# Attention, pooled, then a SiLU block: a new prologue by 256 positions, two seven-product units in the first tile, and loads in another order

## The chip, the core and the metric

One core of a Trainium2 chip runs the whole kernel. The metric is the device time of one execution in microseconds; three runs of the kernel before gave 278.92, 278.94 and 279.31 (median 278.94). A core has five engines that run side by side and meet at semaphores: TensorE (PE: matmuls, with PEld for its weight loads), VectorE (DVE), ScalarE (ACT), GpSimd (POOL) and SyncE (SP). Matmuls write to PSUM, which has eight banks of 512 float32 columns. Transfers between HBM and SBUF are started by SP, ACT and POOL.

## What is computed

```
q, k, v: (8, 8, 576, 64) float32            # batch, head, position, dim
k_p, v_p = mean of k, v over groups of 8 positions     # 72 pooled positions
scores = q @ k_p^T / 8
attn   = softmax(scores)                                # over the 72
x = (attn @ v_p), heads side by side: (4608, 512)
h = x @ w_in                                            # w_in: (512, 2048)
g = h * sigmoid(h)
out = g @ w_out                                         # w_out: (2048, 512), out (4608, 512) float32
```

## The kernel before

The 4608 rows of x are worked in nine tiles of 512. A tile has a first product (x with `w_in`, then SiLU into `h_T`) and a second product (`h_T` with `w_out`, then the store). The attention of batch t+1 is worked inside tile t, so only batch 0 has to be worked ahead of everything; this is the prologue. All is in bfloat16 but for PSUM, the raw k and v and a few sums.

*Order.* The order on each engine is written out by hand: instructions stand on an engine in the order in which the program issues them. Inside a tile a generator `spread` counts steps of PE work, and fillers (attention work, sums, loads) have a step behind which they are issued. An instruction that waits holds all that stands behind it on its engine.

*Banks.* PSUM has the pools "mm" (three banks) and "at" (five).

*Attention of a batch.* k and v come in as rows in five slots of up to 128 rows by 512 float32 (`load_slots`); `slot_sums` adds the eight positions of a group (three adds on DVE for slots 0 to 2, three for 3 and 4); `select_k` and `select_v` bring the sums into place with small matmuls, `copy_k` and `copy_v` take them out of PSUM. `q_transpose` turns q on DVE. `scores` multiplies four heads at a time in four groups of rows of the array, and ACT takes the exponentials (L338) into `es`. `denominators` sums them with a matmul; ACT takes the logarithm (L357) and the exponential of its negative (L358), or DVE the reciprocal (L354). `numerators` multiplies with v (L374), and DVE multiplies with the reciprocal into `xT` (L383). In the prologue this is done in four parts: two groups of four heads (g) by two halves of 288 positions (f). Matmuls on zeros (`warm_up`, L708) stand between the steps.

*First product of tile 0* (`up`). Groups 0 to 10 of 128 columns of `w_in` are worked on the first 288 positions, then on the other 224, then groups 11 to 15 on all 512 (`plain`, L474). The denominators and numerators of the second half stand among the first groups.

*Second product of tile 0* (`down`, L509). Row blocks m = 0, 1, 2 of 128 rows are worked side by side over the 16 groups, then m = 3. The attention of batch 1 stands among them, by thirds of 192 positions.

*Units.* From tile 1 on most of both products is done by seven products of half-blocks instead of eight. They need sums of blocks of x (`unit_x_sum`), of `w_in` (`unit_weight_sum`, one set for each of four units a, b, c, d) and of `w_out` (`weight_sum`); products 1 to 7 go to three banks A, B and E, and DVE and ACT add between them (`behind`). A unit covers four groups. In tile 0 no unit is used; the sums are made in its second product.

*Loads.* k of batch 0 is started by SP and ACT, all else by POOL in this order: q first half, v slots 0 to 2, q second half, v slots 3 and 4, `w_in` columns 0 to 1535 (six transfers), k of batch 1, the last 512 columns of `w_in` (two), q of batch 1, three quarters of `w_out`, v of batch 1, the last quarter of `w_out`.

```python
    act_copy = nc.scalar.copy
    warm_up(9)
...
    q_transpose(0, 0, 0)
    scores(0, part(0, 0))
...
            items = [(g, 0, HS) for g in range(GA)]
            items += [(g, HS, NTT - HS) for g in range(GA)]
            items += [(g, 0, NTT) for g in range(GA, KG)]
            f_up += [(1, lambda: denominators(0, part(0, 1), on_dve=True))]
```

Of the kernel before, what the change touches and what calls it, by code (L numbers as in the profile page):

```python
# [32 lines left out]
ALU = mybir.AluOpType  # L33
# [3 lines left out]
def kernel(  # L37
# [47 lines left out]
    psum = ctx.enter_context(  # L85
        tc.tile_pool(name="psum", bufs=1, space=bass.MemoryType.PSUM)
    )
    ctx.enter_context(tc.manual_schedule())
    banks = dict(mm=3, at=5)

    def ps_tile(shape, dtype, tag, name):
        return psum.tile(shape, dtype, tag=tag, bufs=banks[tag], name=name)
# [18 lines left out]
    w_sum1 = [  # L111
        singles.tile([128, 4, 2, 256], BF16, name=f"w_sum1{n}") for n in range(len(UNITS))
    ]
# [9 lines left out]
    def load_q_half(b, f):  # L123
        for a in range(2):
            es = slice(f * QF * D, (f + 1) * QF * D)
            nc.gpsimd.dma_start(out=batches[b]["q_bf"][:, a, es], in_=q_r[b][:, a, es])
# [22 lines left out]
    def q_transpose(b, a, f):  # L149
        st = batches[b]  # L150
        n = QF * D
        nc.vector.transpose(
            out=st["qT"][:, a, f * QF : (f + 1) * QF]
            .rearrange("r i p c -> r (i p c)").bitcast(FP32),
            in_=st["q_bf"][:, a, f * n : (f + 1) * n].bitcast(FP32),
        )
# [91 lines left out]
    def slot_sums(name, j, halves=False):  # L248
        raw = row_tiles[name][j]
        dst = rows5[name][:, SA:] if j else rows5[name][:, :SA]  # L250
        w = RE // 4 if halves else RE // 2
        while w > D:
            nc.vector.tensor_add(  # L253
                out=raw[..., :w], in0=raw[..., :w], in1=raw[..., w : 2 * w]
            )
            w //= 2
        nc.vector.tensor_add(out=dst, in0=raw[..., :D], in1=raw[..., D : 2 * D])
# [10 lines left out]
    def select_k(b, a):  # L268
        st = batches[b]
        if a == 0:  # L270
            st["kz_ps"] = ps_tile([128, 2, 2, SP], FP32, "at", "kz_ps")
# [26 lines left out]
    def copy_v(b, a, copy=nc.vector.tensor_copy):  # L298
        hs = slice(4 * a, 4 * (a + 1))
# [4 lines left out]
    def part(g, f):  # L304
        return ((g, f * QF, (f + 1) * QF),)
# [16 lines left out]
    def scores(b, segs):  # L322
        st = batches[b]
        w = width(segs)
        sc = [ps_tile([128, 512], FP32, "at", "sc_ps")[:SP, :w] for s in range(4)]
        for g, i0, i1, cs in seg_cols(segs):
            for c in range(2):
                for s in range(4):
# [3 lines left out]
                        lhsT=kz[b % 2][rows, g, c, :],  # L332
                        rhs=st["qT"][rows, g, i0:i1, :, c],
                        start=(c == 0), stop=(c == 1),
                    )
        es = mid.tile([SP, 4, VW], BF16, tag="es", bufs=4, name="es")[:, :, :w]
# [5 lines left out]
    def denominators(b, segs, on_dve=False):  # L342
        st = batches[b]
        w = width(segs)
        es = st["es", segs]
        den_ps = ps_tile([128, 512], FP32, "at", "den_ps")
# [5 lines left out]
        rec = mid.tile([128, VW], FP32, tag="rec", bufs=4, name="rec")[:, :w]  # L352
        if on_dve:
            nc.vector.reciprocal(rec, den_ps[:, :w])  # L354
        else:
            lnd = mid.tile([128, VW], FP32, tag="lnd", name="lnd")[:, :w]
            nc.scalar.activation(lnd, den_ps[:, :w], func=AF.Ln)  # L357
            nc.scalar.activation(rec, lnd, func=AF.Exp, scale=-1.0)  # L358
        st["rec", segs] = rec

    def numerators(b, segs, tags=("at", "at")):
# [6 lines left out]
        rec = st.pop(("rec", segs))  # L368
        nu = []
        for c in range(2):  # L370
            nu_ps = ps_tile([128, 512], FP32, tags[c], "nu_ps")
            for g, _, _, cs in seg_cols(segs):
                for s in range(4):
                    nc.tensor.matmul(  # L374
                        nu_ps[32 * s : 32 * (s + 1), cs],
                        lhsT=st["vp"][:, 4 * g + s, c::2],
# [5 lines left out]
        for c in range(2):  # L382
            nc.vector.tensor_mul(  # L383
                out=xT[:, 2 * g0 + c : 2 * (g0 + ng - 1) + c + 1 : 2, cols],
                in0=nu[c][:, :w].rearrange("r (g n) -> r g n", g=ng),
                in1=rec.rearrange("r (g n) -> r g n", g=ng),
# [41 lines left out]

# [531 lines left out]
```

## Time and profile before

| what | value |
|---|---|
| median of three runs | 278.94 us |
| the profiled execution's own time | 278.04 us |
| its span, from first to last instruction | 276.3 us |
| k of batch 0, slots 0 to 2, summed on DVE | 5.22 to 7.16 us |
| first matmul of the first product | 16.36 us |
| first matmul of the second product of tile 0 | 32.76 us |
| first matmul of tile 1 | 51.03 us |
| bytes moved by DMA, 0 to 60 us | 14.23 MB, 237 GB/s |

A row of the timeline has the start, the duration, the engine, the line, the operation, what it writes and reads, the shape and the count, and in brackets the engine's idle time ahead of it with what ended it; like instructions in a row are merged. A row of the groups has the count, the busy time, the mean ns of one and the idle time ahead. Matmul durations overlap: the pace is read from the distance of their starts. A row of the table of stretches has its bounds, its length, each engine's busy time and count in the order PE, PEld, DVE, ACT, POOL, and then the granted clock of PE, the busy share of the DMA engines and what they moved.

### The profile page before, as it was taken

How to read it: one execution, taken by the hardware profiler on the slowest of the kernel's cores; microseconds unless marked ns; L12 is line 12 of the kernel's file. 1: busy time of each engine (PE TensorE's matmuls, PEld its weight loads, DVE VectorE, ACT ScalarE, POOL GpSimd, SP SyncE). 2: the span in 40 equal slices, each digit the busy share in tenths (PEclk: the TensorE clock that was granted, in tenths of full speed). 3: DMA queues.
4: the chain of work that ended last, by engine and by line, in shares of the span. 5: the costliest groups of instructions: out<-in, count | busy, mean ns of one | idle time of the engine just before them, and what ended most of it. 6: DMA issues, size and time to landing. Idle time of an engine off the chain costs nothing.

```text
span 276.3 us, 7291 instructions
## 1 busy us (share of the span) xinstructions
PE 270.6 (98%) x2959; PEld 211.3 (77%) x2959; DVE 209.7 (76%) x388; ACT 190.7 (69%) x376; POOL 97.3 (35%) x102
## 2 busy tenths in 40 slices
PE   8999999999999999999999999999999999999994
PEld 4348544488788878887888778877887788888883
DVE  4887886887997877877787787768787786766872
ACT  1678766568669785979497958895798578409710
POOL 8756216252138620962087229851900000000000
PEclk9999999999999999999999999999999999999999
DMA  7999999896757896569556966999410032004104
GB/s 211 285 253 246 207 321 180 245 184 117 152 62 147 220 167 116 137 168 169 103 111 170 171 109 159 186 107 132 124 31 0 4 87 67 4 19 110 26 2 152
DMA packets 31473, 37.72 MB, mean 137 GB/s; under 512 B 10352, under 2 KB 22384, under 8 KB 31440
## 3 DMA queue, kind: packets, MB, share of 16 engines
q0 software_dynamic: 23792, 26.64, 52.5%
q1 hardware_dynamic: 7216, 9.97, 13.1%
q10 hardware_dynamic: 432, 0.66, 0.7%
q8 instruction: 23, 0.38, 0.6%
q14 instruction: 10, 0.08, 0.1%
HBM read 36.70 MB, written 9.44 MB: 167 GB/s over the span
## 4 chain that ended last, share of the span: by engine, by line
PE 93%; DVE 4%; DMA 2%; issue 0%; DVEq 0%
PE o_psB L608 16%; PE u_psB L589 15%; PE o_psA L608 10%; PE o_psE L608 10%; PE u_psA L589 10%; PE u_psE L589 10%; PE hp_ps L474 7%; PE sc_ps L330 4%; PE o_ps L509 4%; PE nu_ps L374 3%; PE den_ps L348 2%; DMA raw<-in_k_dram 2%; PE warm_ps L708 1%; DVE xT L383 1%; DVE w_sum L548 1%; DVE raw L253 1%
## 5 line engine op out<-in xcount | busy, mean ns | idle before, releaser
L608 PEld LDWEIGHTS <-h_sum 128*128 128x128 bf16 x512 | 48.4, 98 | 8.8 <-issue 1.2
L589 PEld LDWEIGHTS <-w_sum 128*128 128x128 bf16 x496 | 48.2, 98 | 5.7
L338 ACT ACTIVATE es<-sc_ps 72x384 bf16<-72x384 f32 (+1 forms) x100 | 39.0, 469 | 12.2 <-PE sc_ps L330 12.1
L608 PEld LDWEIGHTS <-h_T 128*128 128x128 bf16 x384 | 36.6, 98 | 6.1 <-issue 1.1
L589 PEld LDWEIGHTS <-w_in_sb 128*128 128x128 bf16 x372 | 36.3, 98 | 4.4
L589 PE MATMUL u_psA<-xT,w_in_sb 128*128 128x256 bf16 x248 | 37.4, 273 | 0.0
L589 PE MATMUL u_psB<-x_sum,w_sum 128*128 128x256 bf16 x248 | 36.7, 273 | 0.0
L608 PE MATMUL o_psB<-w_sum,h_sum 128*128 128x256 bf16 x256 | 32.7, 273 | 0.3 <-DVE o_psE L623 0.3
L608 PE MATMUL o_psA<-w_out_sb,h_T 128*128 128x256 bf16 x256 | 31.9, 272 | 0.0
L618 DVE COPY u_psB<-u_psA 128x512 f32<-128x512 f32 x31 | 21.4, 698 | 10.5 <-PE u_psA L589 10.3
L623 DVE TENSOR_TENSOR u_psE<-u_psB,p 128x512 f32<-128x512 f32 x31 | 20.9, 693 | 9.7 <-ACT p L621 8.6
L627 ACT ACTIVATE h_T<-u_psE 128x512 bf16<-128x512 f32 x31 | 18.5, 598 | 11.2 <-PE u_psE L589 10.9
L383 DVE TENSOR_TENSOR xT<-nu_ps,rec 128x384 bf16<-128x384 f32 (+1 forms) x50 | 23.8, 530 | 0.2
L183 POOL TENSOR_TENSOR raw<-raw 72x1024 f32<-72x1024 f32 x10 | 23.6, 2361 | 0.0
L640 DVE TENSOR_TENSOR c<-u_psB,p 128x512 f32<-128x512 f32 x31 | 21.0, 681 | 3.1 <-PE u_psB L589 2.3
L537 DVE TENSOR_TENSOR h_sum<-h_T 128x1024 bf16<-128x1024 bf16 (+1 forms) x31 | 21.3, 698 | 1.1 <-ACT h_T L627 1.1
L627 ACT ACTIVATE h_T<-u_psB 128x512 bf16<-128x512 f32 x31 | 18.6, 600 | 4.4 <-PE u_psB L589 4.4
L537 DVE TENSOR_TENSOR h_sum<-h_T,h_sum 128x1024 bf16<-128x1024 bf16 (+1 forms) x24 | 20.4, 855 | 0.1
L627 ACT ACTIVATE h_T<-c 128x512 bf16<-128x512 f32 x31 | 19.7, 637 | 0.0
L627 ACT ACTIVATE h_T<-u_psA 128x512 bf16<-128x512 f32 x31 | 18.8, 607 | 1.2 <-PE u_psA L589 1.0
L357 ACT ACTIVATE lnd<-den_ps 128x384 f32<-128x384 f32 (+1 forms) x23 | 11.1, 484 | 11.8 <-PE den_ps L348 11.8
L474 PE MATMUL hp_ps<-xT,w_in_sb 128*128 128x288 bf16 (+2 forms) x124 | 18.9, 304 | 0.1
(87 smaller groups left out, 465.2 us busy)
## 6 DMA issues: line engine op xcount, KB each, us to landing
out_dram<-o_sb SPq DMA_DIRECT2D x128, 64.0 KB, 1.7
raw<-in_k_dram POOLq DMA_DIRECT2D x10, 576.0 KB, 8.2
raw<-in_v_dram POOLq DMA_DIRECT2D x10, 576.0 KB, 7.8
q_bf<-in_q_dram POOLq DMA_DIRECT2D x6, 576.0 KB, 9.1
w_in_sb<-in_moe_w_in_dram POOLq DMA_DIRECT2D x8, 256.0 KB, 8.6
w_out_sb<-in_moe_w_out_dram POOLq DMA_DIRECT2D x4, 512.0 KB, 13.3
raw<-in_v_dram POOLq DMA_DIRECT2D x2, 768.0 KB, 10.9
raw<-in_k_dram POOLq DMA_DIRECT2D x1, 768.0 KB, 10.3
```

The lines of the kernel that those rows point to most:

```text
L183: nc.gpsimd.tensor_add(out=raw[:, :, : 2 * D], in0=raw[:, :, : 2 * D], in1=raw[:, :, 2 * D :])
L338: nc.scalar.activation(es[:, s, :], sc[s], func=AF.Exp, scale=score_scale)
L357: nc.scalar.activation(lnd, den_ps[:, :w], func=AF.Ln)
L383: nc.vector.tensor_mul(out=xT[:, 2 * g0 + c : 2 * (g0 + ng - 1) + c + 1 : 2, cols], in0=nu[c][:, :w].rearrange("r (g n) -> r g n", g=ng), ...
L474: nc.tensor.matmul(hp_ps[:, r0:r1], lhsT=w_in_sb[:, kk, g * 128 : (g + 1) * 128], rhs=xT[:, kk, x0 : x0 + r1 - r0], start=(kk == 0), stop= ...
L537: nc.vector.tensor_tensor(out=h_sum[n][:, k0:k1, :], in0=get(a), in1=get(b), op=op)
L589: nc.tensor.matmul(ps[y, BANK[n]][:, u, :], lhsT=w[:, kk, 128 * u : 128 * (u + 1)], rhs=x[:, kk, :], start=n in (1, 5) and u == 0 and kk == 0,
L608: nc.tensor.matmul(o_bank(n, c), lhsT=left(n, kt, c), rhs=w[:, kt, :], start=n in (1, 5) and kt == 0 and c == 0, stop=kt == KQ - 1, skip_g ...
L618: vcopy(out=ps[y, "B"], in_=ps[y, "A"])
L623: tt(out=ps[y, "E"], in0=ps[y, "B"], in1=f32[y], op=add)
L627: nc.scalar.activation(h_T[:, g : g + 2, j * NQ : (j + 1) * NQ], src, func=AF.Silu)
L640: tt(out=c22, in0=ps[y, "B"], in1=f32[y], op=add)
```

## The change

*Prologue.* Batch 0 is worked in two halves of 256 positions; its last 64 are left over. The scores of a half and of four heads go to two tiles of two banks each, and one exponential is taken over two banks (four heads: two instructions instead of four). The denominators of both groups of heads go to one bank, so that there is one logarithm and one exponential of 512 columns for a half; for the second half as well, where DVE took reciprocals. DVE multiplies into `xT` once for a half and group, 512 wide. All but the three "mm" banks belong to the prologue's own pool first; the pool "at" is opened behind it. Fillers on zeros are 19 instead of 27.

*Sums of k and v.* `slot_sums` is one reduction instead of three adds (two in tile 1).

*The 64 positions left.* Their scores and numerators are appended to the first third of batch 1 (`rest=True`), in wider tiles that lie in `h_sum`.

*First product of tile 0.* Groups 0 to 4 are worked by halves of 256, 5 to 7 by halves into one bank, and groups 8 to 15 as units c and d. The weight sums of unit a stand in the prologue's end, those of c and d in the first product, those of b in the second. In tile 0 a unit's copy from bank A to B is on ACT instead of DVE.

*Second product of tile 0.* It goes over quarters of the groups: all four row blocks over groups 0 to 3, then over 4 to 7, and so on; the parts of m = 3 and m = 0 are taken out once ("e3", "e0") and added at the end. Batch 1's attention stands at other steps. `weight_sum` is cut in two instead of four parts.

*Loads.* POOL starts q's first 256 positions by halves around v, all of `w_in`, the last 64 positions of q, k of batch 1, two quarters of `w_out`, q of batch 1, the third quarter, v of batch 1, the last quarter. *Tile 1:* the k sums, the q transposes and a copy move to other steps, the k copies to ACT.

```diff
-    def slot_sums(name, j, halves=False):
+    def slot_sums(name, j, halves=False, slot=None):
...
-        w = RE // 4 if halves else RE // 2
-        while w > D:
-            nc.vector.tensor_add(
-                out=raw[..., :w], in0=raw[..., :w], in1=raw[..., w : 2 * w]
-            )
-            w //= 2
-        nc.vector.tensor_add(out=dst, in0=raw[..., :D], in1=raw[..., D : 2 * D])
+        w = RE // 2 if halves else RE
+            nc.vector.tensor_reduce(
+                out=dst, in_=raw[..., :w].rearrange("r i (p d) -> r i d p", d=D), axis=AX,
+                op=ALU.add,
+            )
...
+    def scores0(pool, g, f):
+        st = batches[0]
+        sc = [pool.tile([128, 2, 512], FP32, tag="sc2", bufs=2, name="sc_ps") for _ in range(2)]
+        for c in range(2):
+            for s in range(4):
+                rows = slice(32 * s, 32 * (s + 1))
+                nc.tensor.matmul(
+                    sc[s // 2][:SP, s % 2, :NQ],
+                    lhsT=kz[0][rows, g, c, :],
+                    rhs=st["qT"][rows, g, f * IP : (f + 1) * IP, :, c],
+                    start=(c == 0), stop=(c == 1),
+                )
+        es = mid.tile([SP, 4, VW], BF16, tag="es", bufs=4, name="es")[:, :, :NQ]
+        for j in range(2):
+            nc.scalar.activation(
+                es[:, 2 * j : 2 * j + 2, :], sc[j][:SP, :, :NQ], func=AF.Exp,
+                scale=score_scale,
+            )
...
+    def denominators0(den_ps, f):
+        for g in range(2):
+            for s in range(4):
+                nc.tensor.matmul(
+                    den_ps[32 * s : 32 * (s + 1), g * NQ : (g + 1) * NQ],
+                    lhsT=ones, rhs=batches[0]["es", g, f][:, s, :], start=True, stop=True,
+                )
+        nc.scalar.activation(lnd_wide, den_ps, func=AF.Ln)
+
+    def reciprocals0(f):
+        nc.scalar.activation(
+            rec0[:, f].rearrange("r g n -> r (g n)"), lnd_wide, func=AF.Exp, scale=-1.0
+        )
...
+    def x_of(nu, g, f):
+        nc.vector.tensor_mul(
+            out=xT[:, 2 * g : 2 * g + 2, f * NQ : (f + 1) * NQ], in0=nu,
+            in1=rec0[:, f, g : g + 1, :].broadcast_to([128, 2, NQ]),
+        )
...
-                vcopy(out=ps[y, "B"], in_=ps[y, "A"])
+                (acopy if t == 0 else vcopy)(ps[y, "B"], ps[y, "A"])
...
-    for c in range(3):
+    for c in range(4):
         load_w_in(512 * c, 512 * (c + 1))
...
+        warm_up(9)
+        warm_behind(row_tiles["k"][0][:, SA - 1, RE - 128 :], 8)
+        slot_sums("k", 0)
+        kz_ps = one("kz_ps")
+        select_k(0, 0, kz_ps)
+        copy_k(0, 0, nc.scalar.copy)
+        warm_up(3)
+        q_transpose0(0, 0)
+        scores0(pool, 0, 0)
+        slot_sums("k", 1)
+        q_transpose0(1, 0)
+        warm_up(1)
+        select_k(0, 1, kz_ps)
+        copy_k(0, 1)
+        warm_up(2)
+        scores0(pool, 1, 0)
+        warm_up(2)
+        slot_sums("v", 0)
+        den_ps = one("den_ps")
+        denominators0(den_ps, 0)
+        warm_up(1)
+        select_v(0, 0, "mm")
+        copy_v(0, 0, nc.scalar.copy)
+        reciprocals0(0)
+        slot_sums("v", 1)
+        nu = [numerators0(one("nu_ps"), 0, 0)]
+        q_transpose0(0, 1)
+        warm_up(1)
+        select_v(0, 1, "mm")
+        copy_v(0, 1, nc.scalar.copy)
+        q_transpose0(1, 1)
+        x_of(nu[0], 0, 0)
+        scores0(pool, 0, 1)
+        nu.append(numerators0(ps_tile([128, 512], FP32, "mm", "nu_ps"), 1, 0))
+        x_of(nu[1], 1, 0)
+        scores0(pool, 1, 1)
+    load_q_part(0, 2 * IP, QI)
+    for i0, i1 in ((0, 3), (3, 4), (4, 5)):
+        load_slots(nc.gpsimd, 1, "k", i0, i1)
+    load_w_out(0)
+    load_w_out(1)
     load_q(1)
-    for c in range(3):
-        load_w_out(c)
+    load_w_out(2)
...
+    hp0 = [ps_tile([128, 512], FP32, "mm", "hp_ps") for _ in range(3)]
+    for kks in ((0, 1), (2, 3)):
+        for g in range(3):
+            half_group(hp0[g], g, 0, 0, kks)
+    at_pool()
+    den_ps, *nu = (ps_tile([128, 512], FP32, "at", n) for n in ("den_ps", "nu_ps", "nu_ps"))
+    denominators0(den_ps, 1)
+    reciprocals0(1)
+    for n in range(4):
+        unit_weight_sum(0, 1, n)
+    hp0.append(ps_tile([128, 512], FP32, "at", "hp_ps"))
+    half_group(hp0[3], 3, 0, 0, range(KF))
+    moe_tables()
+    for g in range(2):
+        x_of(numerators0(nu[g], g, 1), g, 1)
+    for g in range(4):
+        hidden_half(hp0[g], g, 0)
...
+    FIRST = (
+        "p4.0 p0.1 p1.1 p2.1 g5.0 g6.0 g5.1 g7.0 c1 c5 g7.1 c6 g6.1 c2 c7 d1 c3 d5 c4 d6 cs d2"
+        " p3.1 d7 d3 p4.1 ds d4"
+        " m0:0-4 m1:0-4 m2:0-4 m3:0-4 m0:4-8 m1:4-8 m2:4-8 m3:4-8 e3 m0:8-12 e0 m1:8-12"
+        " m2:8-12 m3:8-12 m1:12-16 m2:12-16 m3:12-16 m0:12-16"
+    )
...
+            for j in range(2):
+                at(83 + j, slot_sums, "v", j)
+                at(97 + j, select_v, 1, j)
+            at(98, copy_v, 1, 0, heads=H)
...
+            for i in range(PW):
+                for n in (1, 2):
+                    at(92 + 7 * i, weight_sum, n, i)
+            sc_at, den_at, nu_at = (72, 84, 95), (84, 95, 106), (103, 106, 110)
...
+            tile_products(0, FIRST, f)
```

In the list FIRST "p" and "g" are half groups (group, then half), "c1" and so on a unit's products, "m1:0-4" row block 1 over groups 0 to 3 of the second product, and "e" the taking out of a part. A half group has two steps, a unit's product two, a row block's part one for each group; the second product starts at step 52 of 116.

## The prediction

> **What bounds the kernel now.** I read the page first, then sums by stage, then the timeline of the first 55 us.
>
> ```profile
> span 276.3 us, 7291 instructions
> PE 270.6 (98%) x2959; PEld 211.3 (77%) x2959; DVE 209.7 (76%) x388; ACT 190.7 (69%) x376; POOL 97.3 (35%) x102
> ```
>
> The reader sees that TensorE is the bound. Stretches (us; busy time and count for PE, its weight loads, DVE, ACT, POOL; then clock, DMA share, GB/s):
>
> ```profile
> 7.20:16.40 9.20, 8.99 (x111) 3.48 (x112) 7.99 (x18) 6.36 (x21) 6.14 (x9) 1.00 1.16 263
> 16.40:32.80 16.40, 16.38 (x158) 10.90 (x157) 12.63 (x26) 12.80 (x31) 7.67 (x11) 1.00 1.18 243
> 32.80:51.30 18.50, 18.50 (x186) 8.37 (x185) 15.13 (x38) 10.74 (x23) 6.30 (x8) 1.00 1.06 245
> ```
>
> These are the rest of the prologue, tile 0's first product and its second. From 16.4 on PE is full. Before 16.4 it is full too, but with matmuls on zeros; there the chain of q, k, v decides. DMA is saturated throughout. The timeline and the form rows:
>
> ```profile
> 5.22 1.55 DVE L253 TENSOR_TENSOR raw<-raw 128x768 f32<-128x768 f32 x2 [2.45 <-DMA raw<-in_k_dram]
> 8.88 1.30 ACT L338 ACTIVATE es<-sc_ps 72x288 bf16<-72x288 f32 x4 [1.04 <-PE sc_ps L330]
> 12.53 1.15 DVE L253 TENSOR_TENSOR raw<-raw 128x512 f32<-128x512 f32 x2 [0.61 <-DMA raw<-in_v_dram]
> 15.59 0.82 DVE L383 TENSOR_TENSOR xT<-nu_ps,rec 128x288 bf16<-128x288 f32 x2
> 16.36 0.41 PE L474 MATMUL hp_ps<-xT,w_in_sb 128*128 128x288 bf16 x2
> 17.06 3.77 DVE L354 RECIPROCAL rec<-den_ps 128x288 f32<-128x288 f32 x2 [0.65 <-PE den_ps L348]
> 32.76 0.59 PE L509 MATMUL o_ps<-w_out_sb,h_T 128*128 128x512 bf16 x2
> 33.75 3.41 PE L509 MATMUL o_ps<-w_out_sb,h_T 128*128 128x512 bf16 x15
> 49.47 1.94 DVE L383 TENSOR_TENSOR xT<-nu_ps,rec 128x384 bf16<-128x384 f32 x4
> 51.03 3.83 PE L474 MATMUL hp_ps<-xT,w_in_sb 128*128 128x512 bf16 x16
> ```
>
> Three marks follow: first product starts at 16.36, second at 32.76, tile 1 at 51.03, where the first 512-column matmul is followed after 0.43 instead of 0.22, so 0.21 is lost to the last xT. The row of 15 gives (3.41-0.38)/14 = 0.216 us for 512 columns, so 0.422 ns a column and 0.109 for 256 with overhead (16 of them span 1.75 in the chain). From 51.3 on nothing of weight changes.
>
> **Prologue, up to the first real matmul.** Durations:
>
> ```profile
> L253 DVE TENSOR_TENSOR raw<-raw 128x768 f32<-128x768 f32 x4 | 3.8, 958 | 4.6 <-DMA raw<-in_k_dram 3.1 <-DMA raw<-in_v_dram 1.4
> L548 DVE TENSOR_TENSOR w_sum<-w_out_sb 128x512 bf16<-128x512 bf16 x8 | 2.8, 416 | 0.0
> L338 ACT ACTIVATE es<-sc_ps 72x384 bf16<-72x384 f32 x12 | 4.8, 480 | 0.0
> L480 ACT ACTIVATE h_T<-hp_ps 128x512 bf16<-128x512 f32 x9 | 5.2, 597 | 1.8 <-PE hp_ps L474 1.8
> L357 ACT ACTIVATE lnd<-den_ps 128x384 f32<-128x384 f32 x3 | 1.5, 492 | 3.5 <-PE den_ps L348 3.5
> ```
>
> *Reduction.* Float32 adds of 768 and 192 elements take 0.96 and 0.36, so 1.04 ns an element plus 0.16. Three adds took 1.94 (5.22 to 7.16). One reduction reads 1536: at the add's rate 1.76. No reduction is in the trace. Bounds: 0.65 ns an input (bf16 adds of 512, one every 0.335) gives 1.16; 1.4 (the f32 transpose, 457 ns for 288 with about 60 of overhead) gives 2.3. I take the add's rate: same data, same engine, same type. A rule speaks against this edit: in the Trainium skill, "VectorE: DVE Perf Modes", section "Rules for kernel authors", a reduction is called the slowest operation of the engine, bound to one element a cycle, to be kept off a hot path. The same page's table has float32 adds at that rate too (2293 ns for 2048, an estimate of 1.72 for 1536), and the adds' row agrees that they are no faster; so by the rule the edit gains about 0.2 here, as by the row, and only on bf16 inputs would it lose.
>
> *Exponentials.* 72x512 over two banks lies between 480 ns (384) and two of 288 (0.69); I take 0.60 as for 128x512, a new one every 0.45. Two take 1.05 instead of 1.30. If it were the two of 288, add 0.2 for each of the four pairs, of which three are on the path: +0.6.
>
> *New wait.* Score banks are used by every half; the next scores wait for the exponentials before. Behind them on PE stands everything.
>
> Step by step: k reduced 5.22-6.98, scores at 8.0 (three idle matmuls instead of four), exponentials to 9.5; the other k sum ends 8.5, selection, copy on DVE to 9.3, scores 9.55, exponentials to 11.0; both denominators 11.35, one logarithm and one exponential of 512 (0.6 each, instead of 1.71 in four) to 12.9. v lands 0.1 earlier than 9.57, since its q load is 128 instead of 144 KB; sums 9.5-11.2 and 11.1-12.35; both v copies on ACT, the second ends 13.7; numerators, xT (512 wide, 0.69) to 13.7 and 14.9. Exponentials of the third scores, behind the copy, end 14.65, fourth scores 14.7, first real matmul at 15.0: -1.36.
>
> **First product.** The two units save 8 of 128 matmuls of 256: 2048 columns, 0.86. So 120x0.109 = 13.1 remain. Denominators and numerators in pairs cost 0.42+0.63; before, with four switches each way, 16.36-20.38 less 18 matmuls of 0.1225 is 1.81: -0.76. But ACT now makes the reciprocals: denominators at 16.4-16.85 (exponentials end 16.2), ln and exp to 18.0, xT 18.7 and 19.4 on DVE. PE reaches the second half at 15.0+12x0.109+0.42+0.44+0.63+0.44 = 18.24, and runs it to 19.62 instead of 18.68: +0.94. The 3.77 of DVE reciprocals, which had 55 matmuls as cover, leave DVE; this cover is what is missing now. The table load (1.28) moves behind the exp, 18.0-19.3; silus follow, and banks come free from 19.7, before they are asked at 20.5. The units bring ACT four copies (0.59) and eight silus of 512 (one every 0.49); with ten half silus (0.27) and three whole ones 10.1 us in the 10.8 up to 30.1, so that no copy is more than 0.1 late by my count; eight fewer zero matmuls cost nothing, they stood in waits. Weight sums: chunk 2 lands near 20.3, chunk 3 near 23.0 (in the trace 17.65+8.6 = 26.2, behind the next k's 768+256+128 KB, which took 3.2), asked for at 22.7 and 26.2. End: 19.62+96x0.109 = 30.1; before, 32.76. In that 2.66 lie 0.60 for two k selections (0.30 each) that only move.
>
> **Second product.** 64x0.216 = 13.8 as before; its other PE work was 18.27-13.8 = 4.45, plus 0.60 selections, plus 0.45 for the 64 left positions (8 more batches of four, wider denominators): 18.9-19.3. Without waits tile 1 would start at 49.4. Waits: POOL issues the same bytes in another order. Four issues, each asked for alone (at 17.65, 18.37, 19.64 and 24.09 us), and their time to landing:
>
> ```profile
> w_in_sb<-in_moe_w_in_dram POOLq DMA_DIRECT2D x1, 256.0 KB, 8.6
> q_bf<-in_q_dram POOLq DMA_DIRECT2D x1, 576.0 KB, 10.7
> w_out_sb<-in_moe_w_out_dram POOLq DMA_DIRECT2D x1, 512.0 KB, 11.9
> raw<-in_v_dram POOLq DMA_DIRECT2D x1, 768.0 KB, 14.8
> ```
>
> So they land at 26.2, 29.1, 31.6 and 38.9: a w_out part takes 2.5. POOL needs 0.56 to 0.78 for an issue and keeps several in flight, so two issues more (batch 0's q in six parts) leave the queue full. q(1), moved behind two w_out parts, lands at 29.1+5.0 = 34.1; DVE transposes it for visit 0 by 35.0 (PE asks at 35.2), and behind it on DVE wait w_sum and the v sums. w_out 0 lands at 28.8 for 30.1. SP's stores change only in order. v's first part has the same bytes ahead, 38.9, and behind it on DVE, in order: both v sums to 41.8, two unit sums, the eviction of row block 0 (to 43.2, needed by PE at 42.95 for its bank), two w_sum of 1024 (0.67 each), the copy of v (to 45.15, needed 45.3). PE then loses 0.25 there and about 0.2 where the next scores take the bank of row block 3 (an ACT copy of 0.59). So waits of 0.45 and tile 1 at 49.85; its first xT is then just ready. In tile 1 the k sums move up, but k's second halves land about 52-53 in either kernel, ahead of the first unit's copy.
>
> **Sum.** -1.36 (prologue), -1.28 (-0.86-0.60-0.76+0.94), +1.50 (0.60+0.45+0.45), -0.21 (the late xT): -1.35 on 276.3. The profiled execution took 278.04, 1.74 around its span; the median of three is 278.94. I take the difference: 277.6.
>
> **Rivals.**
> 1. No wait in the second product, and the late xT covered: -1.9, 277.0. For it: margins there are tenths. Against: DVE has 7.5 us of work between 39.0 and 46.5. 15%.
> 2. The gain is handed back: q(1) or v 1 us later than reckoned, and everything behind them on DVE with it; tile 1 at 50.9, -0.35: 278.6. For it: margins of 0.2 and -0.25. Against: the byte count ahead of v is unchanged. 15%, counting here that the units' copies on ACT stall as much.
> 3. Slower: PE's pace falls to half. The nine zero matmuls up to 5 us are issued every 0.43, later ones every 0.216, at a granted clock of 1.00. Idle fillers after 7 us fall from 18 to 10 and PE waits about 0.5-0.7 at 10.5, 11.7 and 14: if that is enough, 3.8 us at half pace cost 1.9, and small steps 0.4: +0.95, 279.9. Against: no single gap is near the 3.8 that the ramp took. The Trainium skill ("TensorE: Matmul & The Clock Gate", "What's actually happening") says that an idle window of about 3.4 us halves the clock; by it nothing falls, and no run here shows a fall. 10%.
> 4. Slower: the strided reduction takes two cycles an input, 3.36: each pair of sums +2.7, k's and v's in series +5.3 on the 15.0, less the 1.35 and the 0.45 of waits that vanish: +3.5, 282.4. It decides from about 1.4 ns an input on ((1.35+0.45)/5120 inputs above 1.04), so the upper bound of 2.3 stands at no change. 8%.
> 5. The units are not really there: against it, the order of the built instructions has 28 matmuls of 256 for each, so it gets no share.
>
> **How the numbers follow.** Forecast -0.6 to -1.75: 52%, 277.2 to 278.3. A run tells 0.2% (0.56 us) from no change. Faster: 52+15 = 67%; same 15%; slower 18%. Range: down to 276.8, rival 1 with a little of the reduction's lower bound (at 0.65 ns the v sums end 1.0 sooner); up to 279.5, over rival 2, the reduction's and the exponentials' upper bounds; beyond lie rival 4, most of 3, and a few per cent below.
>
> **What would show it.** First product at 15.0 (wrong above 15.8), a gap of 0.9 before its fifth group, second product at 30.1, tile 1 at 49.9; reduction rows of 1.76 and two-bank exponentials of 0.60; v landed by 39, row block 0 evicted by 43.2. If reductions show over 2.3, or zero-matmul spacing is 0.43 after 10 us, the forecast is wrong; if PE is full and tile 1 still starts after 50.7, rival 2.

## The result, and the profile after

The changed kernel is slower: 282.56 us, median of four (282.21 to 282.97), against 278.97; the ratio is 1.0127, with a 95% interval of 1.0109 to 1.0144. Forecast were 277.6 us and a range of 276.8 to 279.5. The profiled execution took 282.21, its span is 280.4; before, 278.04 and 276.3.

| start of | before | forecast | after |
|---|---|---|---|
| first product | 16.36 | 15.0 | 17.88 |
| second product of tile 0 | 32.76 | 30.1 | 34.75 |
| tile 1 | 51.03 | 49.85 | 54.19 |
| length from there to the last matmul | 221.45 | 221.24 | 222.45 |

The page after, its first line and the row of granted clocks:

```profile
span 280.4 us, 7334 instructions
...
PEclk9979999999999999999999999999999999999999
```

The third digit is new: between 14 and 21 us the clock was not full. Two stretches that meet where it changes (length, busy time and count of PE, weight loads, DVE, ACT, POOL; then clock, DMA share, GB/s):

```profile
13.33:16.75 3.42, 2.18 (x37) 1.20 (x37) 3.42 (x6) 1.87 (x6) 1.65 (x4) 1.00 1.23 202
16.75:20.16 3.41, 3.28 (x19) 1.96 (x19) 1.94 (x5) 1.58 (x4) 1.75 (x3) 0.50 1.24 207
```

So TensorE had half its clock for 3.41 us, just when the first product began. In the timeline of TensorE:

```profile
13.55 0.34 PE L301 MATMUL v_ps<-v,shifts 128*128 128x64 bf16 x6 [0.49 <-DVE v L261]
14.34 0.40 PE L372 MATMUL nu_ps<-es,vp 72*32 72x256 bf16 x8 [0.46 <-ACT vp L308]
...
16.82 1.12 PE L338 MATMUL sc_ps<-qT,kz 32*72 32x256 bf16 x8 [0.31 <-ACT es L346]
17.88 2.58 PE L595 MATMUL hp_ps<-xT,w_in_sb 128*128 128x256 bf16 x12
...
22.94 0.38 PE L595 MATMUL hp_ps<-xT,w_in_sb 128*128 128x256 bf16 x2 [0.51 <-DVE xT L380]
23.53 0.70 PE L595 MATMUL hp_ps<-xT,w_in_sb 128*128 128x256 bf16 x5 [0.22 <-DVE xT L380]
```

The twelve first matmuls start 0.21 apart instead of 0.11, and ahead of them TensorE waited up to 0.49 for VectorE and up to 0.46 for ScalarE. VectorE's and ScalarE's timelines show why:

```profile
5.12 2.79 DVE L261 TENSOR_REDUCE k<-raw 128x192 bf16<-128x1536 f32 x1 [2.36 <-DMA raw<-in_k_dram]
8.20 1.85 DVE L261 TENSOR_REDUCE k<-raw 128x128 bf16<-128x1024 f32 x1
10.72 4.60 DVE L261 TENSOR_REDUCE v<-raw 128x192 bf16<-128x1536 f32 x2
...
34.18 3.85 DVE L261 TENSOR_REDUCE k<-raw 128x64 bf16<-128x512 f32 x4
...
41.38 4.64 DVE L261 TENSOR_REDUCE v<-raw 128x192 bf16<-128x1536 f32 x2
```

```profile
9.39 1.08 ACT L346 ACTIVATE es<-sc_ps 72x512 bf16<-72x512 f32 x2 [0.81 <-PE sc_ps L338]
```

A reduction of 1536 inputs takes 2.79, not 1.76, which is over the 2.3 that the prediction named as a sign of being wrong; the exponentials over two banks take the forecast 0.6 each. Both mechanisms of rivals 3 and 4 seem to be at work. Parted by place, the 4.14 us on the span are +1.52 up to the first product, +0.47 in it (the half pace costs 1.1 there, so 0.6 was gained besides), +1.18 in the second product and +0.98 from tile 1 on. There TensorE waits twice for VectorE, which it did not before, behind sums of k and of v:

```profile
56.85 2.44 DVE L261 TENSOR_REDUCE k<-raw 128x192 bf16<-128x768 f32 x2
59.95 0.60 PE L721 MATMUL u_psB<-x_sum,w_sum 128*128 128x256 bf16 x4 [0.39 <-DVE u_psB L750]
76.03 0.28 PE L301 MATMUL v_ps<-v,shifts 128*128 128x64 bf16 x4 [0.49 <-DVE v L261]
```

### The profile page after: what moved, and what is told of

Read it like the earlier page. It is cut to its first block, busy times and chain, and to the rows that moved or that the text cites. A ratio compares the mean times of both kernels' runs of the same rounds, so it can differ in the third digit from the quotient of the medians.

```text
span 280.4 us, 7334 instructions
## 1 busy us (share of the span) xinstructions
PE 270.5 (96%) x2989; PEld 214.3 (76%) x2995; DVE 216.7 (77%) x366; ACT 192.3 (69%) x370; POOL 98.4 (35%) x104
## 4 chain that ended last, share of the span: by engine, by line
PE 87%; DVE 6%; issue 2%; DMA 2%; ACT 1%; DVEq 0%
PE o_psB L740 16%; PE u_psB L721 15%; PE u_psA L721 10%; PE u_psE L721 10%; PE o_psA L740 10%; PE o_psE L740 9%; PE o_ps L636 5%; PE sc_ps L415 3%; PE nu_ps L465 3%; PE den_ps L436 2%; PE hp_ps L595 2%; DMA raw<-in_k_dram 2%; DVE v L261 1%; DVE k L261 1%; PE hp_ps L565 1%
## 5 line engine op out<-in xcount | busy, mean ns | idle before, releaser
L721 PEld LDWEIGHTS <-w_sum 128*128 128x128 bf16 x528 | 51.3, 98 | 7.2 <-issue 1.1
L721 PEld LDWEIGHTS <-w_in_sb 128*128 128x128 bf16 x396 | 38.7, 98 | 4.7
L721 PE MATMUL u_psA<-xT,w_in_sb 128*128 128x256 bf16 x264 | 39.8, 273 | 0.0
L721 PE MATMUL u_psB<-x_sum,w_sum 128*128 128x256 bf16 x264 | 39.1, 272 | 0.4 <-DVE u_psB L750 0.4
L426 ACT ACTIVATE es<-sc_ps 72x384 bf16<-72x384 f32 x80 | 32.2, 482 | 9.7 <-PE sc_ps L415 9.7
L755 DVE TENSOR_TENSOR u_psE<-u_psB,p 128x512 f32<-128x512 f32 x33 | 22.4, 696 | 12.0 <-ACT p L753 8.6
L772 DVE TENSOR_TENSOR c<-u_psB,p 128x512 f32<-128x512 f32 x33 | 22.5, 681 | 3.6 <-PE u_psB L721 2.8
L477 DVE TENSOR_TENSOR xT<-nu_ps,rec 128x384 bf16<-128x384 f32 x40 | 19.8, 548 | 0.4 <-PE nu_ps L465 0.2
L721 PE MATMUL u_psE<-x_sum,w_in_sb 128*128 128x256 bf16 x132 | 19.8, 273 | 0.0
L721 PE MATMUL u_psE<-x_sum,w_sum 128*128 128x256 bf16 x132 | 19.8, 273 | 0.0
```

Of the source, the lines that this page charges most:

```text
L426: nc.scalar.activation(es[:, s, :], sc[s], func=AF.Exp, scale=score_scale)
L477: nc.vector.tensor_mul(out=xT[:, 2 * g0 + c : 2 * (g0 + ng - 1) + c + 1 : 2, xs], in0=nu[c][:, ws].rearrange("r (g n) -> r g n", g=ng), in ...
L721: nc.tensor.matmul(ps[y, BANK[n]][:, u, :], lhsT=w[:, kk, 128 * u : 128 * (u + 1)], rhs=x[:, kk, :], start=n in (1, 5) and u == 0 and kk == 0,
L755: tt(out=ps[y, "E"], in0=ps[y, "B"], in1=f32[y], op=add)
L772: tt(out=c22, in0=ps[y, "B"], in1=f32[y], op=add)
```

## The experiments

Each ratio is to the kernel before, run on the same chip, with its 95% interval; where a result is from one execution, no ratio is given. "Clock" is the mean granted clock of TensorE over an execution, 1.00 being full. Theory: the strided reductions and the fall of the clock are the whole loss. Rivals: one of the two alone, or the new order itself.

### The two failures, each alone

**Adds instead of reductions**, all else as changed:

```diff
-            nc.vector.tensor_reduce(out=dst, in_=raw[..., :w].rearrange("r i (p d) -> r i d p", d=D), ...)
+        while w > D:
+            nc.vector.tensor_add(out=raw[..., :w], in0=raw[..., :w], in1=raw[..., w : 2 * w])
+            w //= 2
+        nc.vector.tensor_add(out=dst, in0=raw[..., :D], in1=raw[..., D : 2 * D])
```

> The changed kernel with every reduction replaced by the float32 adds of before (three for a sum, two on halves), nothing else changed. Theory A (the reduction reads an input in about 1.8 ns, which makes the prologue's sums late, and the late sums make PE idle until its clock falls to half): first real matmul at 15.0 to 15.4 instead of 17.9, second product near 30.5 to 31.5, tile 1 near 50 to 51, median 277.6 to 278.6; the lower figures if the granted clock stays at 1.00, the upper if it falls all the same. Rival B (the new waits on banks and the order of the prologue make it late, and the reduction is a bystander): first real matmul still after 17, median over 281.

Measured: 279.68, ratio 1.0024 (0.9988 to 1.0061), ten executions far apart, and sorted by their mean clock: 277.40, 277.61 and 277.84 at 0.999 to 1.000; 278.82 and 279.19 at 0.994; 280.17 to 280.75 (five) at 0.985 to 0.988. The adds gain 2.9 in the median, and what is left over goes with the clock. The median lies 1.1 above the theory's range, below the rival's; in the profile the first product starts at 15.76, but the clock falls at 15.73, and tile 1 starts at 52.34.

**More matmuls on zeros**, reductions as changed:

```diff
-        warm_up(1)    # ahead of the second selection of k
+        warm_up(3)
-        warm_up(1)    # behind the first denominators
+        warm_up(4)
+        warm_up(2)    # ahead of the first numerators
-        warm_up(1)    # ahead of the second selection of v
+        warm_up(3)
+        warm_up(2)    # ahead of the last scores
```

> The changed kernel with eleven more matmuls on zeros, put where PE waits (two ahead of the second k selection, three behind the first denominators, two ahead of the first numerators, two ahead of the second v selection, two ahead of the fourth scores); reductions kept. Theory A: the granted clock stays at 1.00, the first real matmul stays at about 17.9 (up to 0.3 later), the first twelve take 1.3 instead of 2.5, median 281.3 to 281.8. Rival B (the fall of the clock is without price, the DVE chain decides up to tile 1): median as the changed kernel, 282.5, with a clock of 1.00.

Measured: 280.99, ratio 1.0079 (1.0062 to 1.0096), clock 0.998 to 1.000 in all executions; the twelve first matmuls take 1.21 instead of 2.31. So eleven more zero matmuls make the kernel 1.3 us (by the ratios) to 1.6 us (by the medians) faster. The median lies 0.3 below the theory's range. VectorE's sums of v follow those of k without a wait for the load, although v landed at 10.79:

```profile
10.82 4.63 DVE L261 TENSOR_REDUCE v<-raw 128x192 bf16<-128x1536 f32 x2
```

**Reductions in the kernel before**, nothing else:

```diff
-        while w > D:
...
+            nc.vector.tensor_reduce(out=dst, in_=raw[..., :w].rearrange("r i (p d) -> r i d p", d=D), ...)
```

> The kernel before with the reduction in place of its adds, nothing else changed. Theory A: the sums take 2.8 and 1.85 instead of 1.94 and 1.44, the first v sum ends near 13.2 and the second near 15.3 instead of 14.0, so the first real matmul moves from 16.4 to 17.5 to 18; v's sums in the second product add up to 0.7; median 280.2 to 281.2. Rival B (the reduction has its price only in the new order): 279.0 to 279.5.

Measured: 280.12, ratio 1.0048 (1.0030 to 1.0065), clock full, first product at 18.04 instead of 16.36. The reduction alone, with the old prologue and its 18 zero matmuls, costs 1.3, without any fall of the clock.

**A reduction of neighbours.** Eight neighbouring elements are summed instead of eight that lie 64 elements apart, so other sums, of the same number and shape:

```diff
-                out=dst, in_=raw[..., :w].rearrange("r i (p d) -> r i d p", d=D), axis=AX,
+                out=dst, in_=raw[..., :w].rearrange("r i (d p) -> r i d p", d=D), axis=AX,
```

> The changed kernel with the reduction over eight neighbouring elements instead of eight positions: it sums other elements, in the same number and shape, and reads them with a stride of one. If the stride of 256 bytes is what costs, the first reduction takes about 1.76 instead of 2.79 and the time goes to that of the version with adds; if the operation itself is that slow, 2.79 and the time of the changed kernel, 282.5.

Measured: 277.87 in one execution, clock 1.00. Its VectorE:

```profile
5.33 1.75 DVE L261 TENSOR_REDUCE k<-raw 128x192 bf16<-128x1536 f32 x1 [2.57 <-DMA raw<-in_k_dram]
```

**Elements 8 apart**, so 32 bytes, other sums again:

```diff
+                in_=raw[..., :w].rearrange("r i (x p y) -> r i x y p", x=8, y=8), axis=AX,
```

> The changed kernel with reductions over elements 32 bytes apart (8 float32) instead of 256, the same number and shape; the sums are of other elements. So far 1536 inputs took 2.79 us at 256 bytes and 1.75 at 4 bytes. Theory that any distance costs: about 2.8. Rival that only the far one does: about 1.75.

Measured: 283.54 in one execution; its VectorE:

```profile
5.16 2.92 DVE L261 TENSOR_REDUCE k<-raw 128x192 bf16<-128x1536 f32 x1 [2.39 <-DMA raw<-in_k_dram]
```

Same operation, same number of inputs: 1.75 at 4 bytes (the 1.76 of the forecast), 2.92 at 32 bytes, 2.79 at 256. It is not the operation that is slow but the way it reads, and a distance of 32 bytes is enough. The Trainium skill says so in "Advanced Engine Details and Errata", section "Memory Cachelines": lines of SBUF have 16 bytes, and a stream must hit a line at least twice to run at full rate. Float32 elements read 32 or 256 bytes apart never do so one after the other, and the rows agree. The page gives no price; here it is 1.7 to 1.8 ns an input instead of 1.04 (after taking off 0.16 for each instruction, as for the adds).

### What lets the clock fall

**Fewer zero matmuls in the kernel before**, 8 instead of 18 behind 7.2 us (4, 3, 2, 2, 1, 2, 2, 2 in their places become 3, 1, 2, 0, 0, 1, 0, 1):

```diff
-    warm_up(4)
+    warm_up(3)
...
-    warm_up(3)
+    warm_up(1)
...
-    warm_up(2)
     select_v(0, 0, "mm")
```

> The kernel before with 8 instead of 18 matmuls on zeros between 7.2 and 16.4 us, nothing else changed. By the share of the array in use the window from 11.5 to 14.9 falls from 0.51 to about 0.2. Theory: the clock falls to 0.5 for one window of 3.41 us in most executions, which costs up to 1.7, so that the median rises by 0.8 to 1.7 (279.6 to 280.5); executions whose clock doesn't fall keep 278.9 or gain a tenth. Rival (the fall needs the changed prologue): clock 1.00 and 278.5 to 279.0.

Measured: 280.67, ratio 1.0083 (1.0067 to 1.0099), clock 0.980 to 0.988 in all four executions. In the profile the clock is at half for three windows, where one was expected. Two of its stretches:

```profile
11.00:12.00 1.00, 0.20 (x6) 0.20 (x5) 0.96 (x3) 1.00 (x5) 0.92 (x2) 1.00 1.10 285
12.00:13.00 1.00, 1.00 (x17) 0.32 (x13) 0.14 (x1) 0.97 (x4) 0.31 (x1) 0.50 1.19 183
```

The clock falls at 12.0 without anything of the new prologue; the rival that it needs that is out.

**Adds, and six more zero matmuls** (at the five places of the eleven: one, one, two, one, one), then **the same six on a sixteenth of the array**:

```diff
+    def warm_small(n):
+        for _ in range(n):
+            nc.tensor.matmul(warm_ps[:32], lhsT=warm[:32, :32], rhs=warm[:32], start=True, stop=True)
```

> The changed kernel with adds in place of the reductions and six more matmuls on zeros (128 rows by 128 columns of the array, 512 wide) in TensorE's waits between 8.9 and 15.4 us. Theory (two causes, the strided reduction and the granted clock, and nothing else of weight): with both gone every execution keeps a clock of 1.00 from the first rise on, the twelve first matmuls stand 0.106 us apart, first product at 15.8, second at 31.4, tile 1 at 50.8, and all executions lie at 277.0 to 277.9, about 1.2 below the kernel before (ratio 0.995 to 0.997). Rival (the fall of the clock has nothing to do with the zero matmuls, it comes from the new order of the prologue): executions spread from 277.4 to 280.8 as with the adds alone. Second rival (the new order itself costs): clock 1.00 and still not below the kernel before.

> The same six matmuls on zeros at the same places, 512 wide as well, but on 32 rows by 32 columns of the array instead of 128 by 128, so that TensorE is busy for the same time with a sixteenth of the array. Theory that the clock goes by the share of the array in use within a window of 3.41 us (0.25 and 0.26 in the two windows ahead of a fall seen so far, 0.31 or more ahead of none): the clock still falls in many executions, which spread from 277.3 to 280.8, median above 278.5. Rival that it goes by the time in which TensorE issues nothing: clock 1.00 throughout and the times of the kernel with full-size matmuls, 277.0 to 277.9.

Measured: with full-size ones 278.10, ratio 0.9992 (0.9981 to 1.0003), clock 0.997 or more in all twelve executions; with the small ones 280.05, ratio 1.0060 (1.0036 to 1.0083), nine of twelve executions at 0.994 or less. One window of the small ones, ahead of a fall, and one of the full-size ones, ahead of none:

```profile
13.67:17.09 3.42, 3.20 (x44) 1.26 (x44) 2.82 (x8) 2.13 (x6) 2.21 (x4) 1.00 1.24 204
```

```profile
11.17:14.58 3.41, 2.26 (x23) 0.91 (x22) 3.27 (x7) 1.71 (x4) 3.29 (x5) 1.00 1.21 196
```

TensorE was busy for 3.20 of 3.42 us and lost its clock, and for 2.26 of 3.41 and kept it. Nor is it the longest gap: in the profile with the small ones TensorE idles for at most 0.20 at a time up to the fall, and in that of the kernel before with reductions for 1.09 (at 8.18) without one. So it isn't idle time that counts. What sorts the windows is an estimate from the trace, the share of the array in use: each matmul counts 0.4217 ns for each column that it streams, times the part of the 128 by 128 array that it uses (its rows times its columns of the array), and the sum is taken as a share of the window. All changes of clock lie at multiples of 3.413 us from the first rise, and the phase differs from execution to execution:

```
kernel                    first rise   share of the array in use, window by window
changed                      6.51      0.45 0.34 0.26 | clock falls
adds                         5.49      0.53 0.45 0.25 | falls
adds, second profile         7.24      0.56 0.31 | falls, 0.22 | stays low
adds, third profile          5.20      0.50 0.49 0.27 | falls
adds, six small              6.85      0.45 0.37 0.29 | falls
before, 8 zero matmuls       5.18      0.51 0.23 | falls, 0.21, 0.26 | stays low
elements 8 apart             5.24      0.34 0.45 0.25 | falls, 0.20 | stays low
before                       4.65      0.50 0.63 0.51 0.61, no fall
adds, six full-size          4.34      0.43 0.53 0.40 0.57, no fall
reductions, eleven more      5.37      0.39 0.60 0.71 0.59, no fall
before with reductions       4.62      0.31 0.66 0.38 0.58, no fall
```

Every window up to 0.31 is followed by half the clock, every one from 0.34 on by the full one, but for the last row's first. That one holds float32 matmuls, which start 0.112 us apart where 128 columns by 0.4217 ns are 0.054, and so are counted too low. In the seven profiles not listed no window is below 0.44 before the second product, and the clock never falls. The scores, denominators and numerators of the prologue use 32 by 72 or 72 by 32 of the array, so they count little however busy TensorE is. That the part of the array in use counts is shown by the pair of kernels with six matmuls. Its measure and the border near a third are read from these traces alone; weighted by rows only or by columns only the windows don't sort (the clock falls after up to 0.59, and is full after 0.41 by rows and 0.44 by columns). The Trainium skill ("TensorE: Matmul & The Clock Gate", "What's actually happening") has the free-running window of 3413 ns, as here; its table's condition for the fall, an idle window, isn't what these runs show (3.20 of 3.42 us busy ahead of a fall).

That the phase decides within one kernel is an estimate too. If windows of this length are laid over the first profile with adds from 7 us on, at every phase, the smallest share is 0.23 to 0.34, on both sides of the border; with six full-size ones more it is 0.36 to 0.46, above it at every phase. No profile of an execution of the adds without a fall was taken.

### What is left of the forecast

With both failures out the kernel is within 0.1% of before (0.9992), not 0.5% below. First, chance: the first part of v landed at 9.57 in the profile before and at 9.50 after, but at 11.00 in the one with adds and six zero matmuls, where VectorE waits for it:

```profile
11.03 1.55 DVE L261 TENSOR_TENSOR raw<-raw 128x768 f32<-128x768 f32 x2 [1.23 <-DMA raw<-in_v_dram]
```

Whether the zero matmuls delay it was tried with two further profiles of each of two kernels, unchanged.

> A second profile of the changed kernel with adds. So far the first part of v landed at 9.50 to 9.82 us in the four profiles with the changed prologue and no further zero matmuls, and at 10.22 to 11.00 in the seven with six or eleven more; the bytes moved up to 11 us are equal within 2%. Theory (chance: landings of one kernel spread over this range): this kernel lands anywhere from 9.5 to 11.0. Rival (the zero matmuls delay it): 9.5 to 9.85.

> A second profile of the kernel with adds and six zero matmuls. Chance: v lands anywhere from 9.5 to 11.0. Rival (the zero matmuls delay it): 10.2 to 11.0.

> A third profile of the changed kernel with adds: by chance 9.5 to 11.0, by the rival 9.5 to 9.85.

> A third profile of the kernel with adds and six zero matmuls: by chance 9.5 to 11.0, by the rival 10.2 to 11.0.

Measured: without the zero matmuls 9.82, 11.06, 9.51, with them 11.00, 10.24, 9.57. So either kernel lands over nearly the whole range, and the rival in its strict form is out. A smaller delay isn't: over all profiles of the changed prologue the mean is 9.90 without further zero matmuls (six profiles) and 10.47 with them (nine), too few to tell. The first product moves with the landing: 15.76, 17.52 (the clock had fallen at 14.07), 15.39 and 16.80, 16.03, 15.90. The last profile has v at 9.57, as before, and took 277.89 against 278.04; it is the one to hold the forecast's terms against. Its VectorE, at the end of the sums of v, and its TensorE:

```profile
12.76 0.29 DVE L265 TENSOR_TENSOR v<-raw 128x128 bf16<-128x128 f32 x1
```

```profile
13.25 0.60 PE L845 MATMUL warm_ps<-warm 128*128 128x512 bf16 x2
13.70 0.34 PE L302 MATMUL v_ps<-v,shifts 128*128 128x64 bf16 x6
...
15.15 0.82 PE L339 MATMUL sc_ps<-qT,kz 32*72 32x256 bf16 x8
15.90 1.49 PE L596 MATMUL hp_ps<-xT,w_in_sb 128*128 128x256 bf16 x12
...
19.86 0.38 PE L596 MATMUL hp_ps<-xT,w_in_sb 128*128 128x256 bf16 x2 [0.50 <-DVE xT L381]
20.45 1.25 PE L596 MATMUL hp_ps<-xT,w_in_sb 128*128 128x256 bf16 x10 [0.22 <-DVE xT L381]
```

First product at 15.90 (-0.47), second at 31.64 (15.74 long, -0.65), tile 1 at 51.00 (19.36 long, +1.09). Of the first product's 15.74, three stalls of 0.15 to 0.21 are where a unit's product follows on bank B. The pair from the first profile of this kernel, VectorE's and TensorE's:

```profile
26.21 0.70 DVE L756 TENSOR_TENSOR u_psE<-u_psB,p 128x512 f32<-128x512 f32 x1 [1.39 <-PE u_psB L722]
```

```profile
26.96 0.60 PE L722 MATMUL u_psB<-x_sum,w_sum 128*128 128x256 bf16 x4
```

Between the two products that share the bank stand two others, 0.44 each, and VectorE's sum of 0.70 must be done before the second of the pair can start.

**Without the units.** Groups 8 to 15 as plain groups; the sums of x for tile 0 are left out.

```diff
-        " ... g5.1 g7.0 c1 c5 g7.1 c6 g6.1 c2 c7 d1 c3 d5 c4 d6 cs d2 p3.1 d7 d3 p4.1 ds d4"
+        " ... g5.1 g7.0 g7.1 g6.1 p3.1 p4.1 g8 g9 g10 g11 g12 g13 g14 g15"
```

> The kernel with adds and six zero matmuls, with groups 8 to 15 of the first product as plain groups of 512 instead of the units c and d (their sums of x are left out, their sums of weights are still made for tile 1). The units save 8 of 128 matmuls of 256, 0.86 us, but with them TensorE waits three times 0.15 to 0.20 for VectorE's sum on bank B. Theory (both true): from the first matmul of the first product to the first of the second 16.1 us instead of 15.74, and the median 0.3 to 0.5 higher. By the forecast's step (no stall counted) 16.6 and 0.86 higher. Rival (the units bring nothing): the same or less than with them.

Measured: first product 16.04 long, so the units bring 0.30, not 0.86: the 0.50 of stalls is most of the difference. The median, 278.32 with a ratio of 0.9993 (0.9983 to 1.0003), can't tell the kernel with units from the one without.

**Another order of the first product**, three attempts:

```diff
-        "p4.0 p0.1 p1.1 p2.1 g5.0 g6.0 g5.1 ...
+        "p4.0 p5.0 p0.1 p1.1 p2.1 g6.0 p5.1 ...                          (first)
+        "p4.0 t p2.1 g5.0 g6.0 g5.1 g7.0 c1 c5 g7.1 c6 g6.1 c2 d1 c7 c3 d5 p4.1 c4 d6 cs d2
+         p3.1 m0:0-4 d7 d3 m1:0-4 ds d4 m2:0-4 m3:0-4 ...                (second; t is p0.1 and p1.1 interleaved)
+         p3.1 m0:0-4 d7 d3 m1:0-4 ds d4 m3:0-4 m2:0-4 ...                (third)
```

> The kernel with adds and six zero matmuls, and the first half of group 5 worked ahead of the second half of group 0, so that 0.44 us of matmuls stand in the two waits for the second half's xT (0.50 and 0.22 us at 20.05 and 20.64 where the clock was 1.00). Theory (TensorE waits there for the reciprocals on ScalarE and the product on VectorE, with nothing behind it that comes due sooner): the first wait shrinks to 0.1, tile 1 starts 0.4 earlier and the time falls by 0.3 to 0.45 against the kernel without this. Rival (the wait comes back at the next bank that must be freed): the second product starts at the same time as without it.

Measured: 278.35, ratio 0.9999 (0.9989 to 1.0009). The wait of 0.50 shrinks to 0.07, and 0.39 comes back one bank later, at 22.15, for a silu behind the table load; first to second product 15.85, no gain. (In this order the kernel doesn't compute the reference's output; the number and the shapes of its matmuls are the same.)

> The kernel with adds and six zero matmuls, in another order of the first product: the second halves of groups 0 and 1 are interleaved by pairs of matmuls, so that 0.22 more stand before the second xT of this half is needed, and a third product (d1, then p4.1, then four matmuls of the second product) stands between the products of a unit that share bank B. Theory (the three stalls of 0.15 to 0.20 are the wait for VectorE's sum, 0.70 long, behind two products of 0.44): the stalls go, the wait of 0.22 at the second xT falls below 0.1, first to second product 15.1 where the same work is counted (two times 0.86 us of second-product matmuls now stand ahead of the last unit products), tile 1 starts 0.5 to 0.7 earlier against the first product's start, and the median is 0.5 to 0.7 below the kernel without this order, 0.7 to 1.0 below the kernel before (ratio 0.9965 to 0.9975). Rival (the waits come back, at the next bank or at the copies on ScalarE): within 0.2 of it.

Measured: 278.28, ratio 0.9984 (0.9973 to 0.9996). The three stalls are gone and the second wait too, but a new one of 0.69 stands behind the last unit product, and from the first real matmul to tile 1 it takes 35.24, not less than the 35.10 without this order. The rival holds:

```profile
33.80 0.81 PE L637 MATMUL o_ps<-w_out_sb,h_T 128*128 128x512 bf16 x3 [0.69 <-ACT h_T L762]
```

> The reordered first product with one more step: row block 3 ahead of row block 2 behind the last unit product, since TensorE waited 0.69 us at 33.80 for the bank of row block 2, which the last silu of unit d frees; row block 3 lies in another bank, free by then, and its four matmuls of 0.22 cover that wait. Theory: from the first real matmul to tile 1 34.4 instead of 35.24, median 0.5 to 0.8 below the reordered kernel, 0.8 to 1.2 below the kernel before (ratio 0.9955 to 0.997). Rival (it waits somewhere else again): 35.1 or more and the ratio above 0.998.

Measured: 278.15, ratio 0.9987 (0.9978 to 0.9996), first real matmul to tile 1 34.83 instead of 35.24; of the 0.84 expected, 0.41 came (0.27 against the 35.10 of the old order), and among the rest is a wait of 0.26 at 35.26 for k sums. This version beats the changed kernel, and the one before by 0.13%, where 0.3 to 0.45% was expected; its ratio can't be told from the 0.9992 that the old order has.

## Why the prediction was wrong

The sum by runs, as ratios: 1.0127 for the change, 0.0048 of it the clock (1.0127 less 1.0079), 0.0087 the reductions (1.0079 less 0.9992), the rest -0.0008. In us 1.3, 2.4 and -0.2. Taken out in the other order, the reductions first (1.0127 less 1.0024), it is 0.0103 for them and 0.0032 for the clock: the two overlap, and the intervals are 0.001 to 0.004 to a side.

- *The reduction at 1.76: failed.* The step is "I take the add's rate: same data, same engine, same type". The adds read neighbours, the reduction reads elements 256 bytes apart: 2.79, above the bound of 2.3 too, since both bounds came from rows that read neighbours. Rival 4 named a slow strided read and put it at two cycles an input, 3.36; it had 8%. Its price up to the first product is 1.2 where v lands late (17.79 with eleven zero matmuls and v at 10.79, 16.80 with adds, six, and v at 11.00) and 1.9 where it lands early (15.90 with adds, six, and v at 9.57; the reductions of v could not start before 10.8 anyway, behind those of k). From tile 1 on it is 1.1 (the last matmul of the kernel with reductions and eleven zero matmuls is 2.16 behind that with adds and six, tile 1's start 1.09), where the sum had no term but the late xT.
- *The clock: failed.* The step is the dismissal of rival 3, "no single gap is near the 3.8 that the ramp took". The gaps are not the measure (0.20 at most ahead of one fall, 1.09 without one). The fillers' fall from 18 to 10 was counted there, and "eight fewer zero matmuls cost nothing, they stood in waits" was true of TensorE's time and false of its clock. The rival put 3.8 us at half pace, 1.9, and 0.4 of small steps; measured are one window of 3.41 and a price of 1.3 to 1.6. The two failures seem to feed each other, since the late v sums spread the same matmuls over more windows: the mean clock is 0.988 to 0.993 in all four executions with reductions, and at most 0.994 in seven of ten with adds. No run shows this by itself.
- *What the sum would have been.* In the last profile with adds and six zero matmuls, v at 9.57, the terms are -0.47, -0.65, +1.09 and -0.10, together -0.13 instead of -1.35. (By the same terms rival 1 is -1.80, not the -1.9 it was given.)
- *Prologue, -1.36.* With both out and v at the same landing -0.47. The exponentials (1.08 for two, 1.05 forecast) were right. Of the 0.89 missing, the v sums end at 13.05 instead of 12.35 (adds of 1.9 and 1.4, and a start at 9.74); the rest sits behind that, where the second selection, at 13.70, also stands behind two zero matmuls, one of them the experiment's.
- *First product, -1.28.* The wait for ScalarE's reciprocals and xT, +0.94, was right (0.67 and 0.38 above the plain distance, 1.05 in all). The units' 0.86 was mis-sized: "no copy is more than 0.1 late" looked at ScalarE's copies, and the stalls come from VectorE's sums on bank B; 0.30 is left.
- *Second product, +1.50.* +1.09, 19.36 long in all nine profiles with adds and the second product's order as changed, although v of batch 1 landed anywhere from 38.89 to 40.28: the 0.45 of waits did not come, and rival 2 is out. The late xT (-0.21) is gone at its place, but only 0.10 of it is left at the last matmul.
- *Loads: right.* In the changed kernel's profile w_out's first quarter landed at 28.86 (28.8 forecast), q of batch 1 at 34.24 (34.1), v at 39.00 (38.9).
- *The measure.* The profile before, at 278.04, was 0.9 below its median, so a sum on its span starts from a good execution. In the kernel with adds and six zero matmuls the three profiles with v at 11.00, 10.24 and 9.57 took 278.79, 278.02 and 277.89; whether the landing of v also makes the spread of the other kernels (277.99 to 279.12 in 29 executions of the one before) is not shown.

## What to carry to other kernels

Before three adds become one reduction, look at how far apart the elements lie that it reads one after the other: the trace's price for neighbours does not hold for a stride. Look for a row with the same way of reading, or count with a range that reaches as far as the worst case, as rival 4 did. A matmul on zeros that stands in a wait is not free to remove: count, by windows of 3.4 us and weighted with the part of the array that each matmul uses, what is left to keep the clock. Where a unit of products shares a bank with VectorE's sums, put as much other work between them as the sum takes, then look where the wait goes next.

## What the runs showed of the hardware

A reduction over float32 elements 32 or 256 bytes apart ran at 1.7 to 1.8 ns an input (2.92 and 2.79 us for 1536), over neighbours at 1.04 (1.75 us). The clock of TensorE went to half with TensorE busy for 94% of a window (3.20 of 3.42), in which the matmuls used an estimated 0.29 of the array. Six zero matmuls of 128 by 128 held the clock (0.997 or more in twelve of twelve executions), the same six on 32 by 32 did not (0.994 or less in nine of twelve). With adds alone one kernel's executions spread from 277.4 to 280.75, in step with the mean clock; that the phase of the window decides which it is, is an estimate.
